# Causal attention inside a mixture-of-experts kernel: P turned by query tile, P@V in seven pieces, inverses in two groups

## The chip, the cores and the metric

The kernel runs on one core of a Trainium2 chip. The metric is the time of one execution on the device, in microseconds (us). Engines are named as the profile names them: PE (TensorE, matmuls; PEld its weight loads), DVE (VectorE), ACT (ScalarE), POOL (GpSimd), SP (SyncE, which here issues the DMAs).

## The reference

```python
# q, k, v: (2, 12, 448, 64); float32
scores = q @ k.T / 8, causal mask (-1e9 above the diagonal), minus the row's maximum
attn   = exp(scores); attn /= attn.sum(-1) + 1e-09
x      = (attn @ v) with heads side by side: (896, 768)
# soft mixture of experts, 8 experts x 4 slots
logits = x @ phi                              # (896, 32)
d      = softmax over the tokens (sum + 1e-09); slots = d.T @ x
out_e  = relu(slots_e @ w1[e]) @ w2[e]
x      = softmax over the slots (sum + 1e-09) @ out
# gated layer
out    = ((x @ w_a) * (x @ w_b)) @ w_out      # (896, 768)
```

## The kernel before

The 24 heads are worked in twelve pairs (`it` from 0 to 11). A pair's two heads lie side by side on the 128 partitions, 64 each. The 448 queries are cut into seven query tiles of 64 rows (`i` from 0 to 6); by the causal mask tile i needs 64(i+1) keys. The seven tiles are grouped into four banks, `BANKS = ((6, 0), (5, 1), (4, 2), (3,))`, and each pair is worked in four quarters (`g` from 0 to 3), one bank a quarter. The order is written out by hand: the loop over `it` and `g` at the end of the listing is the order in which each engine gets its instructions, and each engine works its own in that order.

One quarter of pair `it` does this. PE makes the scores of one bank (L266 the mask, L271 the products); DVE takes the rows' maxima (L277); ACT takes the exponentials with their sums (L292, each followed by a short read of the sum). In the first quarter PE also makes P@V of pair it-2 (`pv`, L361). In every quarter PE turns one block of four 128x128 squares of P of pair it-1 (`transp`, L321) into PSUM, from where DVE copies it to the tile pT (L328, L334). `TBLK` lists the sixteen squares (key tile kt, query tile i) in the order in which they lie in pT, and `TORD` says which block of four is turned in which quarter. A square can be turned only when its query tile has been divided by its row sums: DVE adds 1e-9 to the sums (L304) and inverts them (L305), POOL multiplies the tile by the inverses (L308). This is `norm`; it is called in the third quarter for banks 0 and 1, in the fourth for bank 2, and in the first quarter of the next pair for bank 3. In the last pair (11) it is called bank by bank.

POOL has one more task: `begin`, in the second quarter, scales the next pair's queries by 1/8 (L252), once their DMA has landed; the scores of the next pair wait for it.

Beside attention, ACT and DVE convert weights that are packed as 64-bit numbers to 32 bits, three pieces of 768 columns a pair (ACT L168 and L171, DVE L212), and SP loads the next piece into the ring as soon as one is converted. Every third pair PE also makes the logits (L385). When the first six pairs are done, `dispatch0` makes the first half of the softmax over tokens in three parts placed by `DSP`: maxima (PE L400, DVE L401, ACT L405), the turning of the exponentials (PE L411, DVE L413) and their product with x (PE L419, DVE L435). In pairs 10 and 11, and behind them, `keep` has PE multiply the identity into unused places, in counts written by hand (L340).

After attention (131 us on) come the experts, the combination and the gated layer. They load 64 pieces of w1 and w2 through the same ring, and end at 354 us.

Of the kernel before, what the change touches and what calls it, by code (L numbers as in the profile page):

```python
# [17 lines left out]
ALU = mybir.AluOpType  # L18
# [3 lines left out]
S = 448  # L22
# [3 lines left out]
BANKS = ((6, 0), (5, 1), (4, 2), (3,))  # L26
CIX = {6: 0, 0: 1, 5: 2, 1: 3, 4: 4, 2: 5, 3: 6}
POFF = []
_o = 0
for _i in range(7):  # L30
    POFF.append(_o)
    _o += 128 * ((_i + 2) // 2)
PCOLS = _o
TBLK = [(kt, i) for kt in range(4) for i in range(2 * kt, 7)]
NR = 4
NT1 = 32
WPRE = (0,5,20,25)
TORD = (1, 3, 0, 2)
KTORD = (0, 2, 3, 1)
SCQ = 1  # L40
TDVE = (0,1)
TDV2 = (2,3)
TILES = (
    (("rect", 4, 4, 0, 4), ("rect", 8, 4, 0, 8), ("rect", 12, 4, 0, 12), ("tri", 0, 4), ("sq", 0, 8)),
    (("rect", 16, 4, 0, 16), ("rect", 20, 4, 0, 13), ("tri", 4, 2)),
# [2 lines left out]
    (("sq", 8, 16),),  # L48
)
CVOFF = 6  # L50
NRAW = 2
NWARM = 32
NW2 = 4
LAG = 1
CVN = (1,1,0,1)
STAGES = (3, 5)
DSP = ((7, 3), (8, 1), (8, 2))
GROUPS = ((0, 1, 2, 3), (4, 5), (6, 7))
RPOS = (21, 31, 32, 33)
NSEL = 31  # L60
# [28 lines left out]
KEEPV = {10: 12, 11: 6}  # L89
KEEPX = 10  # L90
KEEPT = 24
KEEPE = (2, 3)
KEEPW = 5
KEEPB = (6, 20, 5, 14, 6, 8)
# [3 lines left out]
def moe_kernel(ctx: ExitStack, tc: tile.TileContext, pk, vt, phi, w1, w2, wab, wo, rsel, out):  # L98
    nc = tc.nc
# [19 lines left out]
    for h in range(2):  # L119
        blk = mask16[h * 64:(h + 1) * 64, :]  # L120
        nc.gpsimd.affine_select(
            out=blk, in_=blk, pattern=[[-1, 64]], compare_op=ALU.is_ge, fill=NEG, base=0, channel_multiplier=1,
# [107 lines left out]
    st = {}  # L230
# [54 lines left out]
    def softmax(it, g):  # L285
# [3 lines left out]
        for i, o in zip(tl, (0, 64 * (tl[0] + 1))):  # L289
# [4 lines left out]
                bias=d["nm"][:, c:c + 1], scale=d["scale"], accum_out=d["sm"][:, c:c + 1],  # L294
            )

    def norm(it, tl):
        if not tl:
            return
        d = st[it]  # L300
        lo = CIX[tl[0]]
        p, rc, sm = d["p"], d["rc"], d["sm"]
        r = rc[:, lo:lo + len(tl)]
        nc.vector.tensor_scalar(out=r, in0=sm[:, lo:lo + len(tl)], scalar1=1e-9, scalar2=None, op0=ALU.add)  # L304
        nc.vector.reciprocal(out=r, in_=r)  # L305
        for i in tl:
            n = 64 * (i + 1)
            nc.gpsimd.tensor_scalar(  # L308
                out=p[:, POFF[i]:POFF[i] + n], in0=p[:, POFF[i]:POFF[i] + n],
                scalar1=rc[:, CIX[i]:CIX[i] + 1], scalar2=1.0, op0=ALU.mult, op1=ALU.mult,  # L310
            )
# [26 lines left out]
    def keep(ps, n):  # L338
        for _ in range(n):
            nc.tensor.matmul(  # L340
                ps, lhsT=ident16[:, 0:ps.shape[0]], rhs=ident16[:, 0:ps.shape[1]], start=True, stop=True,
                skip_group_check=True,
            )

    def pv(it):
        d = st[it]
        v = d["v"]
        ps = psV.tile([128, 512], F32, tag="v", name=f"v{it}")
        keep(ps[:, S:512], KEEPV.get(it, 0))
        for kt in KTORD:  # L350
            b0 = TBLK.index((kt, 2 * kt))
            n = 7 - 2 * kt
            if (it, kt) == (10, KTORD[1]):
                keep(psX.tile([128, 128], F32, tag="x", name="idle_x"), KEEPT)
            for h in range(2):
                r = slice(64 * h, 64 * h + 64)
                if kt < 3:
                    lhsT, rhs = v[:, kt, h, :], d["pT"][:, b0:b0 + n, r]
                else:
                    lhsT, rhs = v[0:64, kt, h, :], d["pT"][0:64, b0:b0 + n, r]  # L360
                nc.tensor.matmul(  # L361
                    ps[r, 128 * kt:S], lhsT=lhsT, rhs=rhs, start=(kt == KTORD[0]), stop=(kt == KTORD[3]), skip_group_check=True
                )
        x = ap.tile([128, S], F32, tag="xT", bufs=4, name=f"xT{it}")
        nc.scalar.activation(out=x, in_=ps[:, 0:S], func=AF.Copy)
        xT[it] = x
# [154 lines left out]
    with tc.manual_schedule():  # L521
# [15 lines left out]
        for it in range(13):  # L537
            if 1 <= it < 12:
                load_v(it)
            for g in range(4):  # L540
                if it == 1:
                    warmup(NW2)
                if it < 12:
                    scores(it, g)
                if g == 0 and it >= 2:
                    pv(it - 2)
                if it >= 1:
                    transp(it - 1, TORD[g])
                if step >= CVOFF and CVN[(step + 1) % len(CVN)]:
                    conv_begin(NT1)  # L550
                if it < 12:
                    softmax(it, g)
                if g:
                    if it < 12:
                        norm(it, BANKS[g - 1] if it == 11 else ((), BANKS[0] + BANKS[1], BANKS[2])[g - 1])
                elif it:
                    norm(it - 1, BANKS[3])
                if g == SCQ and it + 1 < 12:
                    begin(it + 1)
                if g == 3 and it + 2 < 12:  # L560
                    load_qk(it + 2)
                if (it, g) in DSP:
                    dispatch0(DSP.index((it, g)))
                if it >= 2 and g == (3 if it == 8 else 1):
                    xtr(it - 2)
                if it in (4, 7, 10) and g == 2:
                    logits((it - 4) // 6, (0, 1, 2) if it != 7 else (3, 4, 5))
                step += 1
                if step > CVOFF:
                    conv_step(CVN[step % len(CVN)], LAG, NT1)  # L570
                if g in TDVE and 1 <= it < 12:
                    evict(it - 1)
# [777 lines left out]
```

## Time and profile before

| | us |
|---|---|
| median of 3 runs | 355.96 |
| lowest and highest | 354.63, 356.37 |
| the profiled execution's own time | 356.16 |
| its span in the trace | 354.1 |

The span runs from the first to the last instruction that the trace shows; what lies around it is 2.06 us. PE is busy for 330.2 us of the span, DVE 214.6, ACT 185.7, POOL 77.4. Times in the rows below are counted from the span's start.

### The profile page before, as it was taken

Reading aid. Unit: us, or ns where it says so; the run is one execution under the profiler, and the core shown is the slowest. Engines: PE = TensorE matmul, PEld = TensorE weight load, DVE = VectorE, ACT = ScalarE, POOL = GpSimd, SP = SyncE. Lnnn points to the kernel's source line nnn. Section 1 sums busy time; section 2 is a strip of 40 time slices with the busy share of each in tenths; the row PEclk is TensorE's granted clock in tenths of the full one; section 3 lists DMA queues with packets and bytes.
Section 4 is the critical chain, followed back from the end, with each engine's and each line's share of the span. In section 5 each row is a group of like instructions: output and inputs, shape, how many; then the busy total and the mean of one; then the engine's idle time right before and its main releaser. Section 6 shows DMA issues by size and latency. Waiting matters only on the chain.

```text
span 354.1 us, 6857 instructions
## 1 busy us (share of the span) xinstructions
PE 330.2 (93%) x2551; PEld 200.9 (57%) x2551; DVE 214.6 (61%) x631; ACT 185.7 (52%) x419; POOL 77.4 (22%) x128
## 2 busy tenths in 40 slices
PE   8899999999999998979987799999899999999996
PEld 5454555545555654423432346634575499989895
DVE  3589999998999842021023877607965799533221
ACT  2499989999898821013036436413644442534321
POOL 2455555554656500010000000000000000121210
PEclk9899999999999999999999989999999999999999
DMA  7759988899799797999999989787920000002122
GB/s 268 308 211 353 327 320 303 322 363 389 290 337 322 260 402 268 420 419 413 418 308 416 417 284 369 252 342 263 423 118 0 3 3 0 0 2 89 44 91 90
DMA packets 20225, 90.52 MB, mean 256 GB/s; under 512 B 2336, under 2 KB 5024, under 8 KB 20192
## 3 DMA queue, kind: packets, MB, share of 16 engines
q1 hardware_dynamic: 20192, 90.09, 67.6%
q8 instruction: 20, 0.33, 0.4%
q14 instruction: 13, 0.11, 0.1%
HBM read 87.33 MB, written 2.75 MB: 254 GB/s over the span
## 4 chain that ended last, share of the span: by engine, by line
PE 65%; DVE 15%; ACT 8%; POOL 4%; DMA 3%; issue 3%; POOLq 0%; ACTq 0%; DVEq 0%
PE M L940 11%; PE o L1240 9%; PE s L271 7%; PE h L669 5%; PE t L321 5%; PE so L710 5%; POOL p L308 4%; PE v L361 4%; DMA raw<-in_wo_dram 3%; ACT p L292 3%; PE ab L796 3%; DVE pf L879 2%; DVE pt L878 2%; PE c L1121 2%; PE hp L689 2%
## 5 line engine op out<-in xcount | busy, mean ns | idle before, releaser
L308 POOL TENSOR_SCALAR p<-p,rc 128x448 f32<-128x448 f32 (+6 forms) x84 | 58.0, 705 | 40.4 <-DVE rc L305 37.2
L271 PE MATMUL s<-qk 64*64 64x448 f32 (+6 forms) x336 | 48.3, 401 | 0.0
L292 ACT ACTIVATE p<-s,nm 128x448 f32<-128x448 f32 (+6 forms) x84 | 39.3, 476 | 13.2 <-DVE nm L282 10.1
L1130 POOL TENSOR_TENSOR cc<-gt,cc 128x512 fp32r<-128x512 f32 (+1 forms) x6 | 6.6, 1101 | 164.5 <-ACT cc L1129 164.5
L940 PE MATMUL M<-wt,P_t 128*128 128x384 f32 x168 | 35.7, 354 | 3.2 <-DVE wt L935 1.2
L321 PE MATMUL t<-ident,p 128*128 128x128 f32 x192 | 32.2, 291 | 4.8 <-POOL p L308 4.7
L277 DVE TENSOR_REDUCE nm<-s 128x1 f32<-128x448 f32 (+6 forms) x84 | 31.9, 415 | 7.4 <-PE s L271 7.1
L940 PEld LDWEIGHTS M<-wt,P_t 128*128 128x128 f32 x168 | 28.9, 191 | 12.4 <-ACT wt L934 4.8
L669 PE MATMUL h<-w,sT 128*32 128x512 f32 x192 | 29.9, 614 | 3.1 <-ACT hs L682 1.6
L321 PEld LDWEIGHTS t<-ident,p 128*128 128x128 f32 x192 | 20.5, 142 | 21.0 <-POOL p L308 10.0
L271 PEld LDWEIGHTS s<-qk 64*64 64x64 f32 x336 | 19.9, 135 | 20.9 <-issue 15.6
L935 DVE TENSOR_TENSOR wt<-wo,wt 128x384 fp32r<-128x384 f32 x48 | 23.8, 552 | 9.6 <-ACT wt L934 9.6
L934 ACT ACTIVATE wt<-wo 128x384 fp32r<-128x384 f32 x48 | 21.8, 512 | 13.5 <-PE M L940 13.1
L361 PE MATMUL v<-pT,v 128*64 128x448 f32 (+3 forms) x192 | 27.2, 398 | 0.0
L710 PE MATMUL so<-w,hpad 128*32 128x384 f32 x256 | 24.6, 493 | 0.9 <-ACT wt L934 0.4
L168 ACT ACTIVATE wab<-raw,shr 128x768 f32<-128x768 int8 x24 | 24.3, 1013 | 0.0
L212 DVE SCALAR_TENSOR_TENSOR wab<-raw,wab 128x768 uint32<-128x768 uint32 x24 | 23.7, 987 | 0.3 <-issue 0.3
L171 ACT ACTIVATE wab<-wab,shr 128x768 int32<-128x768 f32 x24 | 22.6, 941 | 0.0
L1126 DVE TENSOR_TENSOR gt<-gt,c 128x512 f32<-128x512 f32 (+2 forms) x12 | 6.5, 544 | 25.7 <-ACT gt L1125 25.7
L878 DVE TENSOR_TENSOR pt<-abt 128x192 f32<-128x192 f32 (+16 forms) x80 | 18.4, 231 | 3.3 <-ACT abt L838 2.8
L168 ACT ACTIVATE wo<-raw,shr 128x768 f32<-128x768 int8 x12 | 12.2, 1020 | 14.6 <-DMA raw<-in_wo_dram 14.6
L879 DVE TENSOR_TENSOR pf<-abt 128x12 f32<-128x12 f32 (+19 forms) x95 | 19.6, 221 | 0.0
(163 smaller groups left out, 528.7 us busy)
## 6 DMA issues: line engine op xcount, KB each, us to landing
w<-in_w_dram SPq DMA_DIRECT2D x64, 768.0 KB, 8.3
raw<-in_wab_dram SPq DMA_DIRECT2D x24, 768.0 KB, 5.8
raw<-in_wo_dram SPq DMA_DIRECT2D x12, 768.0 KB, 7.2
qk<-in_pk_dram SPq DMA_DIRECT2D x12, 448.0 KB, 5.6
v<-in_pk_dram SPq DMA_DIRECT2D x12, 192.0 KB, 5.7
out_dram<-ost SPq DMA_DIRECT2D x6, 384.0 KB, 2.3
v<-in_vt_dram SPq DMA_DIRECT2D x12, 32.0 KB, 5.5
out_dram<-ost SPq DMA_DIRECT2D x2, 192.0 KB, 1.9
```

The lines of the kernel that those rows point to most:

```text
L168: nc.scalar.activation(out=dst, in_=top, func=AF.Prelu, bias=shr[:, 0:1], scale=1.0, alpha=2.0 ** -40)
L271: nc.tensor.matmul(sb[r, o:o + n], lhsT=qT[r, 64 * i:64 * i + 64], rhs=kT[r, 0:n], start=False, stop=True, skip_group_check=True,)
L277: nc.vector.tensor_reduce(out=d["nm"][:, c:c + 1], in_=sb[:, o:o + 64 * (i + 1)], axis=AX.X, op=ALU.max, negate=True)
L292: nc.scalar.activation(out=d["p"][:, POFF[i]:POFF[i] + n], in_=sb[:, o:o + n], func=AF.Exp, bias=d["nm"][:, c:c + 1], scale=d["scale"], ac ...
L308: nc.gpsimd.tensor_scalar(out=p[:, POFF[i]:POFF[i] + n], in0=p[:, POFF[i]:POFF[i] + n], scalar1=rc[:, CIX[i]:CIX[i] + 1], scalar2=1.0, op0 ...
L321: nc.tensor.transpose(ps[:, j, :], d["p"][:, o:o + 128], ident)
L361: nc.tensor.matmul(ps[r, 128 * kt:S], lhsT=lhsT, rhs=rhs, start=(kt == KTORD[0]), stop=(kt == KTORD[3]), skip_group_check=True)
L669: nc.tensor.matmul(ps[32 * g:32 * g + 32, :], lhsT=sT[:, 0, c, :], rhs=wt[8 * e + i // 3][:, 512 * (i % 3):512 * (i % 3) + 512], start=(i ...
L710: nc.tensor.matmul(so[32 * g:32 * g + 32, 0:384], lhsT=t[:, c, :], rhs=wt[8 * e + 4 + i // 4][:, 384 * (i % 4):384 * (i % 4) + 384], start ...
L879: nc.vector.tensor_tensor(out=view(p), in0=ops[0][0], in1=ops[0][1], op=ALU.mult)
L940: nc.tensor.matmul(mps[k][h][:, 0:384], lhsT=l[:, f, :], rhs=r, start=(n == 0 and i == 0), stop=(n == 11 and i == 2))
L1240: nc.tensor.matmul(ops[t][h][:, 0:384], lhsT=hl[k // 2][:, l, k % 2, o], rhs=mhl[k][:, r, 384 * h:384 * h + 384], start=(k == 0 and i == 0 ...
```

## The change

- `TBLK` puts the sixteen squares in another order, and `TORD` turns them in the order 3, 2, 1, 0: first the four squares of query tile 6, then those of tiles 5 and 1, of 4 and 0, of 2 and 3.
- `pv` works off the list `PVL`: seven pieces for each head in place of four. A piece is one key tile with one, two or three query tiles, which lie one square or four squares apart in pT. The columns that go through are 1024 a head, before and after.
- `NORMS` has two groups: banks 0 and 1 (inverted in the third quarter, as before), and banks 2 and 3 together (in the next pair's first quarter).
- In pairs 0 to 10 the 1e-9 is added by POOL (`guard`), right behind the exponentials of the second and of the fourth quarter, and no more by DVE.
- The three parts of the first dispatch stand at (8, 0), (8, 1), (8, 3) in place of (7, 3), (8, 1), (8, 2).
- In pair 10 the 24 filling matmuls stand ahead of the sixth piece of P@V; before, ahead of the second of four.

```diff
-TBLK = [(kt, i) for kt in range(4) for i in range(2 * kt, 7)]
+TBLK = (
+    (0, 2), (0, 3), (1, 2), (1, 3), (0, 4), (1, 4), (2, 4), (0, 0), (0, 5), (1, 5), (2, 5), (0, 1), (0, 6), (1, 6),
+    (2, 6), (3, 6),
+)
+PVL = ((0, 4, 3, 4), (1, 5, 3, 4), (2, 6, 3, 4), (3, 15, 1, 1), (0, 7, 2, 4), (0, 0, 2, 1), (1, 2, 2, 1))
...
-TORD = (1, 3, 0, 2)
-KTORD = (0, 2, 3, 1)
+TORD = (3, 2, 1, 0)
...
+NORMS = ((), BANKS[0] + BANKS[1], (), BANKS[2] + BANKS[3])
...
-DSP = ((7, 3), (8, 1), (8, 2))
+DSP = ((8, 0), (8, 1), (8, 3))
...
+    def guard(it, tl):
+        if tl and EPSLO <= it < 11:
+            c = slice(CIX[tl[0]], CIX[tl[0]] + len(tl))
+            nc.gpsimd.tensor_scalar(
+                out=st[it]["rc"][:, c], in0=st[it]["sm"][:, c], scalar1=1e-9, scalar2=0.0, op0=ALU.add, op1=ALU.add
+            )
...
-        nc.vector.tensor_scalar(out=r, in0=sm[:, lo:lo + len(tl)], scalar1=1e-9, scalar2=None, op0=ALU.add)
+        if it == 11 or it < EPSLO:
+            nc.vector.tensor_scalar(out=r, in0=sm[:, lo:lo + len(tl)], scalar1=1e-9, scalar2=None, op0=ALU.add)
         nc.vector.reciprocal(out=r, in_=r)
...
-        for kt in KTORD:
-            b0 = TBLK.index((kt, 2 * kt))
-            n = 7 - 2 * kt
-            if (it, kt) == (10, KTORD[1]):
+        for kt, b0, n, by in PVL:
+            i = TBLK[b0][1]
+            if (it, b0) == (10, KEEPP):
                 keep(psX.tile([128, 128], F32, tag="x", name="idle_x"), KEEPT)
+            k = slice(0, 128 if kt < 3 else 64)
             for h in range(2):
                 r = slice(64 * h, 64 * h + 64)
...
                 nc.tensor.matmul(
-                    ps[r, 128 * kt:S], lhsT=lhsT, rhs=rhs, start=(kt == KTORD[0]), stop=(kt == KTORD[3]), skip_group_check=True
+                    ps[r, 64 * i:64 * (i + n)], lhsT=v[k, kt, h, :], rhs=d["pT"][k, b0:b0 + by * (n - 1) + 1:by, r],
+                    start=(kt == 0), stop=(b0 in (15, 7, 2)), skip_group_check=True,
                 )
...
+                if it < 12:
+                    guard(it, NORMS[g])
                 if g:
                     if it < 12:
-                        norm(it, BANKS[g - 1] if it == 11 else ((), BANKS[0] + BANKS[1], BANKS[2])[g - 1])
+                        norm(it, BANKS[g - 1] if it == 11 else NORMS[g - 1])
                 elif it:
-                    norm(it - 1, BANKS[3])
+                    norm(it - 1, BANKS[3] if it == 12 else NORMS[3])
```

What the diff does to POOL shows in the rows of one pair. These are POOL's of pair 3 before (qk_478 are the queries of pair 4, p_137 is P, rc the inverses, sm the sums; the last number is the operand's shape):

```order
L252 TENSOR_SCALAR qk_478<-qk_478 128x448
L308 TENSOR_SCALAR p_137<-p_137,rc_424 128x448
L308 TENSOR_SCALAR p_137<-p_137,rc_424 128x64
L308 TENSOR_SCALAR p_137<-p_137,rc_424 128x384
L308 TENSOR_SCALAR p_137<-p_137,rc_424 128x128
L308 TENSOR_SCALAR p_137<-p_137,rc_424 128x320
L308 TENSOR_SCALAR p_137<-p_137,rc_424 128x192
L308 TENSOR_SCALAR p_137<-p_137,rc_424 128x256
```

And the same pair after:

```order
L306 TENSOR_SCALAR rc_427<-sm_426 128x4
L258 TENSOR_SCALAR qk_477<-qk_477 128x448
L322 TENSOR_SCALAR p_137<-p_137,rc_427 128x448
L322 TENSOR_SCALAR p_137<-p_137,rc_427 128x64
L322 TENSOR_SCALAR p_137<-p_137,rc_427 128x384
L322 TENSOR_SCALAR p_137<-p_137,rc_427 128x128
L306 TENSOR_SCALAR rc_427<-sm_426 128x3
L322 TENSOR_SCALAR p_137<-p_137,rc_427 128x320
L322 TENSOR_SCALAR p_137<-p_137,rc_427 128x192
L322 TENSOR_SCALAR p_137<-p_137,rc_427 128x256
```

The first add stands ahead of the scaling of the next pair's queries, and the second between the two groups of tiles.

On PE the first quarter of pair 5 reads thus before, from the scores on (v is P@V of pair 3, t_1 the first block that is turned of pair 4; behind each row stand the engines that it waits for):

```order
L271 MATMUL s_0_721<-qk_593 64x448 [waits DMAHW2_49,Pool_49]
L271 MATMUL s_0_721<-qk_593 64x448
L271 MATMUL s_0_721<-qk_593 64x64 x2
L361 MATMUL v_729<-pT_621,v_484 64x448 [waits DMAHW6_49,DVE_49]
L361 MATMUL v_729<-pT_621,v_484 64x448
L361 MATMUL v_729<-pT_621,v_484 64x192 x2
L361 MATMUL v_729<-pT_621,v_484 64x64 [waits DMAHW7_49]
L361 MATMUL v_729<-pT_621,v_484 64x64
L361 MATMUL v_729<-pT_621,v_484 64x320 [waits DVE_49]
L361 MATMUL v_729<-pT_621,v_484 64x320
L321 MATMUL t_1_741<-ident,p_132 128x128 [waits PE_49,Pool_49]
L321 MATMUL t_1_741<-ident,p_132 128x128 x2
```

After:

```order
L277 MATMUL s_0_728<-qk_596 64x448 [waits DMAHW2_49,Pool_49]
L277 MATMUL s_0_728<-qk_596 64x448
L277 MATMUL s_0_728<-qk_596 64x64 x2
L371 MATMUL v_736<-pT_630,v_483 64x192 [waits DMAHW6_49,DVE_49]
L371 MATMUL v_736<-pT_630,v_483 64x192 x5
L371 MATMUL v_736<-pT_630,v_483 64x64 [waits DMAHW7_49]
L371 MATMUL v_736<-pT_630,v_483 64x64
L371 MATMUL v_736<-pT_630,v_483 64x128 x2
L371 MATMUL v_736<-pT_630,v_483 64x128 [waits DVE_49]
L371 MATMUL v_736<-pT_630,v_483 64x128 x3
L335 MATMUL t_3_754<-ident,p_132 128x128 [waits PE_49,Pool_49]
L335 MATMUL t_3_754<-ident,p_132 128x128 x3
```

Eight products have become fourteen, with three waits in both, and the block that is turned next is number 3 (tile 6 alone) where it was number 1 (tiles 4, 5, 6 and 2).

The first part of the dispatch has moved on PE. After the change its row stands here, in the first quarter of pair 8 (lt; before, it stood ahead of the scores of that pair, s_0):

```order
L371 MATMUL v_1099<-pT_991,v_844 64x128 x3
L335 MATMUL t_3_1117<-ident,p_137 128x128 [waits PE_49,Pool_49]
L335 MATMUL t_3_1117<-ident,p_137 128x128 x3
L411 MATMUL lt_1129<-lsb,selsum 128x448 [waits Activation_49]
L272 LDWEIGHTS ident_81
L272 MATMUL s_1_1139<-mask_83,ident_81 128x2x64
L277 MATMUL s_1_1139<-qk_957 64x384 x2
L277 MATMUL s_1_1139<-qk_957 64x128 x2
L335 MATMUL t_2_1147<-ident,p_137 128x128 [waits PE_49,Pool_49]
L335 MATMUL t_2_1147<-ident,p_137 128x128 x2
L335 MATMUL t_2_1147<-ident,p_137 128x128 [waits Pool_49]
L422 MATMUL dps_1159<-ident,lsb 112x32 [waits Activation_49]
```

Between lt and the turning of its exponentials (dps) PE now has one bank of scores and one block to turn; before, it had two banks of scores, P@V and two blocks.

## Rows read from the trace of the kernel before

**Rows 1.** Busy time by engine, granted clock and DMA, in stretches of the span.

```profile
20.72:29.54 8.82, 8.82 (x71) 4.85 (x68) 8.37 (x21) 8.66 (x22) 5.13 (x8) 1.00 0.95 349
29.54:39.05 9.51, 8.91 (x70) 4.86 (x68) 9.16 (x21) 9.12 (x24) 5.55 (x8) 1.00 0.94 341
...
49.56:58.33 8.77, 8.77 (x71) 4.87 (x68) 8.27 (x20) 7.76 (x19) 4.93 (x8) 1.00 0.88 317
...
131.00:190.00 59.00, 52.05 (x516) 23.40 (x514) 9.92 (x27) 11.51 (x18) 1.91 (x9) 1.00 0.98 378
```

**Rows 2.** What PE waited for, 5 to 131 us: total, times, longest.

```profile
PE t L321 <- POOL p L308: 4.7, 6, 1.7
```

**Rows 3.** Timeline of PE around the first quarter of pair 6.

```profile
57.25 0.65 PE L271 MATMUL s<-qk 64*64 64x256 f32 x4
...
58.48 1.08 PE L271 MATMUL s<-qk 64*64 64x448 f32 x8
59.49 2.25 PE L361 MATMUL v<-pT,v 128*64 128x448 f32 x16
62.33 0.73 PE L321 MATMUL t<-ident,p 128*128 128x128 f32 x4 [0.59 <-POOL p L308]
```

**Rows 4.** Timeline of PE at the first transposition, pair 1.

```profile
10.67 1.08 PE L271 MATMUL s<-qk 64*64 64x448 f32 x8
13.48 0.97 PE L321 MATMUL t<-ident,p 128*128 128x128 f32 x4 [1.73 <-POOL p L308]
...
14.92 1.97 PE L271 MATMUL s<-qk 64*64 64x384 f32 x8
```

**Rows 5.** Busy time as in rows 1, of the two stretches at half clock.

```profile
13.68:17.09 3.41, 3.41 (x19) 1.97 (x18) 0.84 (x2) 0.38 (x3) 1.17 (x3) 0.50 0.56 212
...
204.84:208.20 3.36, 3.36 (x11) 1.26 (x11) 3.36 (x19) 0.94 (x2) 0.00 (x0) 0.50 0.75 309
```

**Rows 6.** Timeline of DVE at the start: the first add of 1e-9.

```profile
10.51 0.17 DVE L304 TENSOR_SCALAR rc<-sm 128x4 f32<-128x4 f32 x1
```

**Rows 7.** DVE's adds by form, 5 to 131 us: total, mean ns, idle before.

```profile
L304 DVE TENSOR_SCALAR rc<-sm 128x2 f32<-128x2 f32 x14 | 4.9, 353 | 0.4 <-ACT p L292 0.3
...
L304 DVE TENSOR_SCALAR rc<-sm 128x1 f32<-128x1 f32 x12 | 1.7, 141 | 0.0
```

**Rows 8.** POOL's smallest operation, by form, 5 to 131 us.

```profile
L308 POOL TENSOR_SCALAR p<-p,rc 128x64 f32<-128x64 f32 x12 | 4.6, 383 | 0.0
```

**Rows 9.** POOL's scaling of the queries: ns shortest, median, longest.

```profile
L252 POOL TENSOR_SCALAR qk<-qk x10: 566/567/1257, 16.0 to 107.6; 128x448 f32<-128x448 f32 x10
```

**Rows 10.** Timeline of ACT, pair 5: the last sum of the second quarter.

```profile
56.90 0.21 ACT L292 ACTIVATION_READ_ACCUMULATOR p<-s,nm 128x1 f32 x1
```

**Rows 11.** Timeline of DVE, pair 5: an add, and a conversion behind it.

```profile
60.21 0.53 DVE L304 TENSOR_SCALAR rc<-sm 128x2 f32<-128x2 f32 x1
...
60.86 1.01 DVE L212 SCALAR_TENSOR_TENSOR wab<-raw,wab 128x768 uint32<-128x768 uint32 x1
```

**Rows 12.** Timeline of PE, the last pair's blocks.

```profile
122.19 1.40 PE L321 MATMUL t<-ident,p 128*128 128x128 f32 x8
...
123.86 1.17 PE L321 MATMUL t<-ident,p 128*128 128x128 f32 x8
```

**Rows 13.** Timeline of PE, DVE and ACT at the first dispatch.

```profile
78.38 0.96 PE L400 MATMUL lt<-lsb,selsum 128*128 128x448 f32 x2
...
79.93 0.60 DVE L401 TENSOR_REDUCE smalls<-lt 128x1 f32<-128x448 f32 x1
...
80.76 0.63 ACT L405 ACTIVATE lsb<-lt,smalls 128x448 f32<-128x448 f32 x1 [0.33 <-DVE smalls L428]
```

**Rows 14.** Timeline of SP's loads at the end of attention.

```profile
113.61 12.83 SPq L494 DMA_DIRECT2D w<-in_w_dram  x8
```

**Rows 15.** The chain that ended last, its longest piece.

```profile
176.78 11.54 DMA raw<-in_wo_dram
```

**Rows 16.** Timeline of POOL, pair 5's first six tiles.

```profile
58.71 3.97 POOL L308 TENSOR_SCALAR p<-p,rc 128x448 f32<-128x448 f32 x6 [2.04 <-DVE rc L305]
```

More of the change, by code (lines that the diff above doesn't have):

```diff
@@ L50 @@
 CVOFF = 6
+EPSLO = 0
 NRAW = 2
@@ L91 @@
 KEEPT = 24
+KEEPP = 0
 KEEPE = (2, 3)
@@ L349, in pv @@
         keep(ps[:, S:512], KEEPV.get(it, 0))
-        for kt in KTORD:
-            b0 = TBLK.index((kt, 2 * kt))
-            n = 7 - 2 * kt
-            if (it, kt) == (10, KTORD[1]):
+        for kt, b0, n, by in PVL:
+            i = TBLK[b0][1]
+            if (it, b0) == (10, KEEPP):
                 keep(psX.tile([128, 128], F32, tag="x", name="idle_x"), KEEPT)
+            k = slice(0, 128 if kt < 3 else 64)
             for h in range(2):
                 r = slice(64 * h, 64 * h + 64)
[L357 to L360, printed above, removed]
                 nc.tensor.matmul(
-                    ps[r, 128 * kt:S], lhsT=lhsT, rhs=rhs, start=(kt == KTORD[0]), stop=(kt == KTORD[3]), skip_group_check=True
+                    ps[r, 64 * i:64 * (i + n)], lhsT=v[k, kt, h, :], rhs=d["pT"][k, b0:b0 + by * (n - 1) + 1:by, r],
+                    start=(kt == 0), stop=(b0 in (15, 7, 2)), skip_group_check=True,
                 )
```

## The prediction

> **What bounds the kernel now.** I began with the busy time stretch by stretch, a stretch being one pair of heads. Read PE's column against the stretch's length: pair 2 takes 8.82 us with PE busy for all of it, pair 5 takes 8.77 and is full too; pair 3 does the same work and takes 9.51 with PE busy for 8.91 [rows 1]. DVE and ACT stand close behind (9.16 and 9.12 of 9.51), but where PE has no hole the pair is 0.7 us shorter, so PE's row sets the pace of attention and its holes are what can be won. Next I asked what those holes wait for. From 5 to 131 us there is one answer: the first transposition waits for POOL's division of P, six times, 4.7 us in all, the longest 1.7 [rows 2]. The timeline shows the place: scores, P@V, 0.59 us of nothing, then the turning [rows 3]. The five short holes (pairs 3, 4, 6, 7, 10) make 3.0 us together, 0.6 each; the long one is the first transposition of all [rows 4]. They arise because the block turned first holds squares of tiles 4, 5, 6 and 2, and so needs six of the seven tiles divided.
>
> The granted clock is the last view: two stretches stand at 0.50, that is 1.2 GHz in place of 2.4 [rows 5]. The first runs from 13.68 to 17.09, 0.2 us after the end of the 1.73 us in which PE stood idle [rows 4].
>
> **The change, part by part.**
>
> The first block now holds tile 6 alone, the first that POOL divides. In the quarter of rows 3 POOL begins that tile at 58.71 [rows 16]; even at 1.26 us, the longest that it takes for 448 columns [rows 9], it is done by 60.0, and PE asks for it when P@V ends, at 61.74 [rows 3]. So all five short holes close at this place: 3.0 us. The later blocks need tiles 5 and 1, then 4 and 0, then 2 and 3. The second group of inverses comes a quarter later than before, but its first square is wanted only two blocks (0.7 us each) and two banks of scores (1.08 each) after the quarter begins, 3.5 us on PE [rows 3], against a reciprocal and three POOL operations of 0.4 to 0.6 us [rows 8, 9]. I price that at nothing; a DVE that comes to the reciprocal 1.5 us late would cost what is over.
>
> At the start the hole is 1.73 us. DVE's first add began at 10.51 [rows 6]; on POOL it begins there too. The add itself is not in this trace on POOL. Bounds: not under DVE's 0.14 us [rows 7], not over POOL's smallest tile, 0.38 on average [rows 8]; I take 0.3, near the second, since it is the same engine and kind of operation with fewer columns. Then a reciprocal (as short as DVE's other small operations, 0.2), two hand-overs (0.2 to 0.3 together) and the first tile at 0.57, as the scaling of the same 448 columns [rows 9]: ready at 11.8 to 12.0. The scores end at 11.75 [rows 4]. About 0.3 us of wait stays; **1.4 us** is won.
>
> The half clock behind it: in it eight score matmuls take 1.97 us instead of 1.08 [rows 4]; the whole 3.41 us hold 1.7 us of delay [rows 5]. With no long idle ahead, the clock has no cause to fall. I take **1.6 us**, leaving 0.1 for filling matmuls that nobody waits for.
>
> The removed DVE work is three adds and one of three reciprocals a pair, about 0.8 us (0.17, 0.35 and 0.14 for the adds [rows 6, 7], 0.15 for the reciprocal by the same measure). It is off PE's path, and buys only slack on an engine that was 96% busy (9.16 of 9.51 [rows 1]). I price it at nothing; without that cover it would be worth up to 0.8 us a pair, which the full PE excludes.
>
> POOL's first add of a pair stands ahead of the scaling of the next pair's queries, and PE's next scores wait for that scaling. This is where the closed holes can partly come back. In pair 5, full as it is, ACT's last sum of the second quarter is read at 57.11 [rows 10], and the next scores that read the scaled queries start at 58.48 [rows 3]: 1.37 us. Into it go the add (0.3, bounds 0.14 and 0.38), the scaling (0.57) and hand-overs (0.1 to 0.3): 0.97 to 1.17, so it fits, with little to spare. Queued behind the add on POOL is that scaling, then the first tile; whoever waits is PE. ACT's own work is nearly a full pair long too (9.12 of 9.51), so with the holes gone it can fall somewhat further back. I charge 0.1 us for each of the five closed holes: 3.0 becomes **2.5 us**.
>
> Here a row speaks against the change: the scaling, 0.57 us as a rule, once took 1.26, and an add on DVE took 0.53 where another took 0.17, with POOL working beside it [rows 6, 9, 11]. The Trainium skill (Advanced Engine Details and Errata, VectorE Performance Modes) says why: VectorE's second port into SBUF is shared with GpSimd, so that two-port VectorE instructions and GpSimd's block each other. By that rule the adds that leave DVE stop being blocked, and the ones that come to POOL can be; the trace agrees with the blocking. I charge nothing for it in the forecast, since by the loop no conversion of DVE stands in the second quarter; it is the third rival.
>
> P@V has seven pieces a head instead of four, the columns unchanged. What a piece costs beside its columns: one piece of 256 columns takes 0.65 us, two pieces of 512 take 1.08, so 256 columns and one piece more are 0.43 [rows 3]. From this, four pieces with 1024 columns would be 1.94; P@V takes 2.25. If the 0.31 left over belongs to the four pieces, it is 0.08 a piece, three more are 0.23 a pair, 2.8 us in twelve pairs. If it belongs to the three places where PE waits for a semaphore, which are three before and after, it is nothing. Bounds 0 and 2.8; I take 0, since the waits can be read in the order of the instructions, and a price for a piece in no row by itself.
>
> The last pair's first two blocks took 1.40 us, the other two 1.17 [rows 12]; the difference is the wait for POOL that the new order drops: **0.2 us**. The filling matmuls, the loads and their counts stay.
>
> The dispatch: between the start of its first part (lt) and the turning of the exponentials PE now has 0.96 us of lt itself, scores of 1.08 and 0.7 of turning [rows 3], 2.6 us. The chain beside it is lt 0.96, DVE 0.60 and a small operation of 0.15, ACT 0.63 and a read of 0.2 [rows 7, 10, 13], 2.5 with no queue on either engine. I charge **0.2 us**; free at best, and 1 us if ACT comes a conversion late.
>
> **The sum.** 1.4 + 1.6 + 2.5 + 0.2 - 0.2 = 5.5 us. It lies wholly before 131 us and must carry to the end. From 131 to 190 us the DMAs are busy 98% [rows 1], and the longest single piece of the chain, 11.54 us, is a load [rows 15]. So the stream of weights matters there. It begins with eight loads at 113.61 [rows 14] that go out as attention's conversions free the ring: earlier attention, earlier stream. I carry all of it. The profiled execution took 356.16 us, 0.2 over the median of 355.96; taken off the median, 350.5.
>
> **Rivals.**
>
> 1. The second half-clock stretch goes as well. It is 3.36 us [rows 5], worth 1.7. For it: the three runs lie 354.63 to 356.37, 1.74 apart, as if one run had been without one such stretch. Against: the work around it is unchanged. Time 348.8.
>
> 2. The closed holes come back behind the scaling, or behind the landing of the queries' DMA; PE is then full nowhere more than before, and start, clock and tail remain: 5.5 - 2.5 = 3.0, time 353.0. For it: 0.2 us of spare. Against: a DVE with less to do reaches the maxima sooner.
>
> 3. Slower: DVE's conversions hold POOL during both add and scaling, each 0.69 us longer (1.26 less 0.57 [rows 9]). The 1.0 to 1.2 us become 2.4 to 2.6 against 1.37: 1.1 us on each of ten pairs, 11 us, against the 3.0 that closed holes give and 3.0 from start, clock and tail: 361. It decides against the kernel from 0.6 us a pair. Against: DVE's conversions come in the other three quarters, so only a DVE that has drifted would do it.
>
> 4. P@V pays for its pieces, 2.8 us: 353.3.
>
> 5. The stream of weights, not attention, sets the rest: no change, 356. For it: the 98%. Against: in attention the DMAs move 317 to 349 GB/s, and 378 behind it [rows 1], so they wait there for the ring.
>
> **How the numbers follow.** A measurement of this kernel tells about 0.5% (1.8 us) from no change. Forecast 0.50, rival 1 0.15, rival 2 0.13, rival 4 0.08, rival 5 0.07, slower 0.07. Forecast and rivals 1, 2, 4 are faster by over 1.8 us, save the edges of 2 and 4: 0.84. Same 0.09, slower 0.07. The range leaves out rivals 3 and 5 and a little of each edge: 348.2 to 353.7. The likeliest case alone spans 349.5 to 351.8, from the bounds of the start, the scaling and the dispatch.
>
> **What would show it.** PE's waits for POOL at the transposition gone, or 0.3 us at the first; the stretch from 13 to 17 us at full clock; pairs without logits at 8.8 to 8.9 us all along; P@V still about 2.25 us; lt and its turning without a hole between them over 0.3 us; the experts beginning some 5.5 us sooner and the 11.5 us load no longer. It is wrong if PE shows new waits ahead of a pair's first scores, if P@V grows, or if the experts start early and end no earlier.

## The result, and the profile after

The changed kernel took 350.78 us (median of 4 runs, 349.99 to 351.46) against 355.38 (354.63 to 356.37) beside it: a ratio of 0.9868, interval 0.9831 to 0.9906. Measured twice more in the sets below, the same kernel gave 0.9892 (0.9855 to 0.9928) and 0.9882 (0.9843 to 0.9921), so the change is worth 1.1 to 1.3%, 3.8 to 4.7 us. Executions that lie over 1.5% above the fastest of their kernel are left out of ratios and medians: one of the kernel before (359.11) and one of the changed kernel (354.49), both in the sets below. The profiled execution took 351.46 with a span of 349.4; before it was 356.16 and 354.1.

First PE's waits from 5 to 131 us (total, times, longest), against [rows 2]. In the changed kernel L335 is the turning of P, L277 the scores, L258 POOL's scaling of the queries, L411 and L422 lt and the turning in the dispatch:

```profile
PE s L277 <- POOL qk L258: 1.1, 1, 1.1
PE dps L422 <- ACT es L416: 0.9, 1, 0.9
PE s L277 <- DMA qk<-in_pk_dram: 0.4, 1, 0.4
PE lt L411 <- ACT lsb L401: 0.2, 1, 0.2
```

The turning waits for POOL nowhere. New are a wait of 1.1 us ahead of a pair's scores and one of 0.4 for pair 1's queries. (The 0.9 stands behind the last pair, and was there before.) The stretches of pairs 2 to 5 and of the experts, to be read as [rows 1]:

```profile
17.73:26.52 8.79, 8.79 (x83) 5.60 (x81) 8.10 (x18) 8.79 (x22) 5.77 (x11) 1.00 0.97 350
26.52:36.47 9.95, 8.86 (x83) 5.59 (x81) 9.40 (x20) 9.67 (x25) 6.73 (x11) 1.00 0.94 342
36.47:46.24 9.77, 9.77 (x86) 5.77 (x87) 8.50 (x17) 9.25 (x22) 6.77 (x11) 1.00 0.97 352
46.24:55.03 8.79, 8.79 (x82) 5.60 (x81) 7.73 (x17) 7.91 (x20) 5.27 (x11) 1.00 0.92 340
131.00:190.00 59.00, 52.89 (x497) 22.38 (x500) 10.23 (x24) 14.75 (x23) 1.91 (x9) 0.97 1.00 388
...
13.68:17.09 3.41, 3.41 (x35) 2.18 (x31) 2.95 (x9) 2.36 (x10) 1.89 (x5) 1.00 0.55 205
177.03:180.44 3.41, 3.07 (x20) 0.99 (x24) 1.86 (x3) 2.18 (x3) 0.00 (x0) 0.50 1.00 290
200.92:204.33 3.41, 3.41 (x11) 1.75 (x12) 3.06 (x14) 0.94 (x2) 0.00 (x0) 0.50 0.73 221
```

These stretches, from a pair's first scores to the next pair's, begin at the product; those of [rows 1] begin 0.15 us earlier, at the mask. The first and the fourth are full at 8.79 us; 9.77, in the third, is a pair with logits, and full too; the second has the new hole. The lower three rows answer to [rows 5]: the stretch that stood at half clock now has the full 1.00, and behind 131 us there are two stretches at half clock where there was one.

PE's timeline: the first transposition, against [rows 4]; pair 6's first quarter, against [rows 3]; the last pair, against [rows 12]; the first matmul of the experts (L682):

```profile
10.90 1.08 PE L277 MATMUL s<-qk 64*64 64x448 f32 x8 [0.41 <-DMA qk<-in_pk_dram]
11.91 0.66 PE L335 MATMUL t<-ident,p 128*128 128x128 f32 x4
...
12.78 1.08 PE L277 MATMUL s<-qk 64*64 64x384 f32 x8
...
55.03 1.08 PE L277 MATMUL s<-qk 64*64 64x448 f32 x8
56.04 2.26 PE L371 MATMUL v<-pT,v 128*64 128x192 f32 x28
58.24 0.66 PE L335 MATMUL t<-ident,p 128*128 128x128 f32 x4
...
116.88 1.09 PE L335 MATMUL t<-ident,p 128*128 128x128 f32 x8
...
118.31 1.16 PE L335 MATMUL t<-ident,p 128*128 128x128 f32 x8
...
132.59 2.78 PE L682 MATMUL h<-w,sT 128*32 128x512 f32 x24
```

The transposition follows the scores without a hole, 1.57 us sooner than at 13.48 and at full clock. P@V takes 2.26 us for 28 matmuls where 16 took 2.25. The experts begin at 132.59; before, the same matmul began at 138.13. That is 5.54 us sooner, where the sum said 5.5.

The chain that ended last (start, length, what) shows where the new hole comes from, and what became of the gain behind 131 us:

```profile
27.65 7.66 DMA qk<-in_pk_dram
...
35.46 0.96 POOL qk L258
36.42 0.04 issue
36.47 1.08 PE s L277 x8
...
171.23 12.36 DMA raw<-in_wo_dram
```

Pair 4's queries land 7.66 us after their issue; only then can POOL scale them, and the scores wait for that. The load that was the chain's longest piece, 11.54 us [rows 15], is issued 5.55 us sooner and takes 12.36, so it lands 4.73 us sooner. 4.7 is also what the span has lost: 0.8 of the 5.5 us is given back here. The row from 131 to 190 doesn't say why, since before, its first 7.1 us lie ahead of the experts. Counted from the first expert matmul, in the form of [rows 1], first before and then after, up to the load's issue and while it is under way:

```profile
138.13:176.78 38.65, 35.56 (x332) 15.39 (x333) 4.00 (x13) 5.85 (x10) 1.91 (x9) 1.00 1.01 415
176.78:188.32 11.54, 10.20 (x112) 4.09 (x113) 2.85 (x4) 3.13 (x3) 0.00 (x0) 1.00 1.02 333
...
132.59:171.23 38.64, 35.55 (x332) 15.39 (x333) 4.00 (x13) 5.85 (x10) 1.91 (x9) 1.00 1.01 415
171.23:183.59 12.36, 10.62 (x101) 4.02 (x102) 2.83 (x4) 3.21 (x3) 0.00 (x0) 0.86 1.02 332
```

The DMAs are as busy and move data at the same rate in both, so fuller DMAs are not what makes the load longer. What differs in these rows is the granted clock, 0.86 in place of 1.00: the new stretch at half clock, from 177.03, lies within the load.

### The profile page after: what moved, and what is told of

Same layout as the page of the kernel before. It is cut to its first block, busy times and chain, and to the rows that moved or that the text cites. A ratio compares the mean times of both kernels' runs of the same rounds, so it can differ in the third digit from the quotient of the medians.

```text
span 349.4 us, 7132 instructions
## 1 busy us (share of the span) xinstructions
PE 329.3 (94%) x2695; PEld 209.2 (60%) x2695; DVE 207.8 (59%) x587; ACT 184.7 (53%) x419; POOL 83.7 (24%) x150
## 4 chain that ended last, share of the span: by engine, by line
PE 72%; DVE 12%; DMA 8%; ACT 4%; issue 1%; POOL 1%; SPq 1%; ACTq 0%; DVEq 0%; POOLq 0%
PE M L953 12%; PE s L277 10%; PE o L1253 9%; PE v L371 7%; PE t L335 6%; PE h L682 5%; PE so L723 5%; DMA qk<-in_pk_dram 4%; DMA raw<-in_wo_dram 4%; PE ab L809 3%; DVE pf L892 2%; DVE pt L891 2%; PE c L1134 2%; PE hp L702 2%; DVE pf L903 2%; PE xt L384 1%
## 5 line engine op out<-in xcount | busy, mean ns | idle before, releaser
L322 POOL TENSOR_SCALAR p<-p,rc 128x448 f32<-128x448 f32 (+6 forms) x84 | 59.0, 718 | 10.9 <-DVE rc L319 10.2
L277 PE MATMUL s<-qk 64*64 64x448 f32 (+6 forms) x336 | 47.2, 394 | 1.6 <-POOL qk L258 1.1
L277 PEld LDWEIGHTS s<-qk 64*64 64x64 f32 x336 | 19.6, 133 | 22.0 <-issue 15.0
L682 PE MATMUL h<-w,sT 128*32 128x512 f32 x192 | 29.9, 613 | 2.1 <-ACT hs L695 1.6
L335 PE MATMUL t<-ident,p 128*128 128x128 f32 x192 | 31.1, 286 | 0.0
L371 PE MATMUL v<-pT,v 128*64 128x192 f32 (+2 forms) x336 | 27.4, 299 | 0.0
L335 PEld LDWEIGHTS t<-ident,p 128*128 128x128 f32 x192 | 20.1, 141 | 11.4 <-issue 7.1
L371 PEld LDWEIGHTS v<-pT,v 128*64 128x64 f32 (+1 forms) x336 | 19.2, 135 | 6.0 <-issue 2.8
L809 PE MATMUL ab<-wab,sT 128*32 128x384 f32 x192 | 20.0, 523 | 0.5 <-DVE sT L647 0.5
```

The source lines that it names most:

```text
L277: nc.tensor.matmul(sb[r, o:o + n], lhsT=qT[r, 64 * i:64 * i + 64], rhs=kT[r, 0:n], start=False, stop=True, skip_group_check=True,)
L322: nc.gpsimd.tensor_scalar(out=p[:, POFF[i]:POFF[i] + n], in0=p[:, POFF[i]:POFF[i] + n], scalar1=rc[:, CIX[i]:CIX[i] + 1], scalar2=1.0, op0 ...
L335: nc.tensor.transpose(ps[:, j, :], d["p"][:, o:o + 128], ident)
L371: nc.tensor.matmul(ps[r, 64 * i:64 * (i + n)], lhsT=v[k, kt, h, :], rhs=d["pT"][k, b0:b0 + by * (n - 1) + 1:by, r], start=(kt == 0), stop= ...
L682: nc.tensor.matmul(ps[32 * g:32 * g + 32, :], lhsT=sT[:, 0, c, :], rhs=wt[8 * e + i // 3][:, 512 * (i % 3):512 * (i % 3) + 512], start=(i ...
L809: nc.tensor.matmul(abps[q][32 * g:32 * g + 32, 0:384], lhsT=sT[:, 1, c, :], rhs=w[:, c % 2, 384 * g:384 * g + 384], start=(c == 0), stop=( ...
```

## The experiments

No kernel here leaves out any of the work. Ratios are to the kernel before, beside them on the same chip: the first four are one set (before 354.49), the next three another (354.24), the last four a third (356.06).

**The order of the squares alone** (`TBLK`, `TORD`, `PVL` as changed; the rest as before):

```diff
-EPSLO = 0
+EPSLO = 11
-NORMS = ((), BANKS[0] + BANKS[1], (), BANKS[2] + BANKS[3])
+NORMS = ((), BANKS[0] + BANKS[1], BANKS[2], BANKS[3])
-DSP = ((8, 0), (8, 1), (8, 3))
+DSP = ((7, 3), (8, 1), (8, 2))
```

Expected: 

> The new order of turning and the seven pieces alone: 1e-9 added by DVE, inverses in three groups and the dispatch as before. Theory (PE sets the pace, and its holes came from the block that was turned first): PE waits for POOL at the transposition no more than 0.3 us in all, the stretch behind 13 us at full clock, the experts' first matmul at 132.5 to 133.3 us (138.1 before, 132.6 after the whole change), time 350.3 to 351.6 us. Rival (DVE, 96% busy, has to be relieved of its adds for the holes to close): holes of 0.3 us or more in most pairs, the experts begin at 135 us or later, time 353 us or more.

Measured: 351.2 us, ratio 0.987 (0.9822 to 0.9917), and no wait of the turning for POOL (`EPSLO = 11` leaves the adds on DVE). The experts begin at 133.46, a little later than expected; PE waits twice for the scaling of the queries, 1.3 us in all. That is the whole gain. The adds, the two groups and the place of the dispatch add nothing that can be told.

**Everything but the order** (old `TBLK`, `TORD`, four pieces; adds on POOL, new dispatch). The old first block needs tile 2 of bank 2, which two groups would divide too late; so this kernel keeps three groups, and POOL makes three adds a pair:

```diff
-TORD = (3, 2, 1, 0)
+TORD = (1, 3, 0, 2)
-NORMS = ((), BANKS[0] + BANKS[1], (), BANKS[2] + BANKS[3])
+NORMS = ((), BANKS[0] + BANKS[1], BANKS[2], BANKS[3])
```

Expected: 

> The whole change but for the order of turning, which with its four pieces is as before; inverses in three groups, since the old order needs tiles 4 and 2 a quarter earlier; 1e-9 by POOL, dispatch at the new quarters. Theory: the holes at the first transposition are back, six or more, 4.5 to 6 us in all, with half clock after the first; experts begin at 137.5 to 138.7 us, time 354.5 to 356.5 us, though DVE has less to do. Rival (relief of DVE): holes under 0.3 us each, experts begin at 133 to 135.5 us, time 351 to 353 us.

Measured: 375.62 us, ratio 1.0543 (1.0476 to 1.0611). I had not foreseen 20 us of loss. PE's waits, in the view of the first fence (L332 is here the turning, L319 POOL's scaling of P):

```profile
PE t L332 <- POOL p L319: 16.5, 9, 2.7
```

Before, it was 4.7 in six [rows 2]. POOL's timeline in pair 3 (L303 is the add of 1e-9, L255 the queries):

```profile
32.84 0.56 POOL L255 TENSOR_SCALAR qk<-qk 128x448 f32<-128x448 f32 x1
34.66 0.42 POOL L303 TENSOR_SCALAR rc<-sm 128x2 f32<-128x2 f32 x1 [1.26 <-ACT p L295]
35.17 2.67 POOL L319 TENSOR_SCALAR p<-p,rc 128x448 f32<-128x448 f32 x4
37.92 0.23 POOL L303 TENSOR_SCALAR rc<-sm 128x1 f32<-128x1 f32 x1
38.25 2.16 POOL L319 TENSOR_SCALAR p<-p,rc 128x320 f32<-128x320 f32 x3
```

POOL stands idle for 1.26 us until ACT has the sums of bank 2, with the four tiles of banks 0 and 1 queued behind the add; DVE had made their inverses by 34.1, so they lose the last 0.5 us of it and the add's own time. Then the add of bank 3 (37.92) stands ahead of the two tiles of bank 2, which the turning is waiting for. The turning starts at 39.60 after 2.05 us of nothing. There is more half clock too: the granted clock is 0.50 from 14.42 for 6.83 us, and from 51.97, 86.10 and 120.24 for 3.41 each; before there was one such stretch ahead of 131 us. 11.8 us more of waits, and half of 13.7 us more at half clock, make 18.6; the experts begin 20.0 us later than before (158.17).

**The same with the adds behind the scaling** in POOL's queue, to test that reading:

```diff
-                if it < 12:
-                    guard(it, NORMS[g])
                 if g:
...
                     norm(it - 1, BANKS[3] if it == 12 else NORMS[3])
+                if it < 12:
+                    guard(it, NORMS[g])
```

Expected: 

> The old order of turning with three groups and the adds on POOL (375.6 us), with one thing changed: each add stands in POOL's queue behind the scaling of the bank before it, not ahead of it. The same instructions, in another order on one engine. Theory: of the 20 us most come from the queue: the add of bank 3 waits for ACT's sums (1.26 us idle at 34.66) with four ready tiles behind it, and the next add stands ahead of the two tiles that the transposition wants. With the adds behind, the hole falls from 2.05 us to between 0.6 (as with the adds on DVE) and 1.3, the clock stays full in attention, and the time is 355 to 364. Rival: the way from POOL over DVE's reciprocal and back to POOL costs the time, wherever the add stands: then the hole stays near 2 us and the time above 370.

Measured: 357.66 us, ratio 1.0112 (1.0035 to 1.0189), the hole 1.03 us, and the clock full from 4.85 to 161.87. The turning still waits 7.5 us in eight waits. (The add that waits for ACT's sums at 34.66 is that of bank 2.) The same instructions in another order on one engine are worth some 18 of the 20 us, what half clock costs among them: the theory holds. The hole keeps 0.4 us over before's 0.59 [rows 3]; the way from POOL over DVE's reciprocal and back has a price too.

**The new order with three groups on POOL**, the fourth corner:

```diff
-NORMS = ((), BANKS[0] + BANKS[1], (), BANKS[2] + BANKS[3])
+NORMS = ((), BANKS[0] + BANKS[1], BANKS[2], BANKS[3])
```

Expected: 

> The changed kernel, but with the inverses in three groups (the third bank, tiles 4 and 2, apart from the fourth, tile 3), so that POOL has three adds a pair, and the add of the fourth bank stands in POOL's queue ahead of the scaling of tiles 4 and 2. With the old order of turning the same groups and adds gave 375.6 us and nine waits of the transposition for POOL. Theory: those waits came because the block turned first needed tiles 4 and 2; in the new order they are wanted only by the third and fourth block, two quarters later, so no transposition waits and the time is that of the changed kernel, 350 to 353. Rival: three adds on POOL are slow by themselves, because its queue waits for ACT's sums three times a pair and the scaling of the queries is behind it: then the next scores wait, a pair takes 10 us or more, and the time is above 358.

Measured: 350.22 us, ratio 0.9867 (0.9819 to 0.9915), no wait of the turning. (Pair 1's scores wait 1.58 us for their queries and a stretch at half clock follows, from 11.72; the experts begin at 133.70.) What costs 20 us under the old order costs nothing under the new one, since the late tiles are wanted two quarters later.

**The adds back on DVE** (`EPSLO = 11`, the rest as changed):

```diff
-EPSLO = 0
+EPSLO = 11
```

Expected: 

> The whole change, but 1e-9 is added by DVE in all pairs, in two groups. Theory: DVE is off PE's path, so nothing changes by more than 0.4 us: experts begin at 132.3 to 133.0 us, time within 0.7 us of the whole change run beside it. Rival (DVE's adds blocked by POOL reach PE, 0.4 to 0.8 us a pair in eleven pairs): experts begin 2 us or more later, time 353 us or more.

Measured: 349.99 us, ratio 0.9852 (0.9806 to 0.9899), against 0.9892 (0.9855 to 0.9928) for the changed kernel beside it: the intervals overlap. The median is 1.6 us lower and the experts begin at 131.69, sooner than I expected (0.7 us and 132.3): in this profile the hole at pair 4 is 0.3 us. That the adds on POOL cost something is not shown, nor excluded.

**The changed kernel again**, in that set:

Expected: 

> The whole change once more, unaltered, to see what repeats. The experts should begin at 132.4 to 132.8 us again; the time should lie at 350 to 351.5 us. If the spread behind 131 us goes with stretches at half clock, the runs with the lower mean clock are the longer ones, 1.7 us for each 3.4 us stretch; if they are off the path, the clock says nothing of the time.

Measured: 351.55 us (348.74 to 353.7, 9 runs). The executions with the lower mean clock are the longer ones: 348.81 us at 1.0, 348.74 to 350.53 at 0.995, 351.55 to 352.13 at 0.990, 352.41 and 353.7 at 0.985. (The ten others of this kernel, those of the result and of its third run, are less well ordered: 349.99 to 351.35 at 0.988, 354.21 at 0.990.) The profiled execution was the longest, 353.7, and shows one way in which executions differ: PE's timeline at the start,

```profile
9.71 0.22 PE L272 MATMUL s<-mask,ident 128*128 128x128 bf16 x1
11.49 1.37 PE L277 MATMUL s<-qk 64*64 64x448 f32 x4 [1.56 <-DMA qk<-in_pk_dram]
```

and the stretch behind it, as in [rows 5]:

```profile
11.93:15.34 3.41, 3.41 (x21) 2.12 (x19) 1.69 (x5) 1.02 (x4) 1.56 (x5) 0.50 0.96 369
```

Pair 1's queries came 1.56 us late and the clock fell; the experts begin at 134.76, 2.17 us later than in the first profile. So the half clock at the start can still come, by another wait; it did so in two more profiles, of the kernels with three groups and with the load moved.

**The first hole filled** in the kernel before:

```diff
                 if it == 1:
                     warmup(NW2)
...
+                if (it, g) == (1, 0):
+                    warmup(28)
                 if it >= 1:
                     transp(it - 1, TORD[g])
```

Expected: 

> The kernel before, with nothing changed but 28 filling matmuls on PE ahead of the first transposition, where PE stood idle for 1.73 us (11.75 to 13.48); four such matmuls take 0.22 us at full clock, so they take about 1.55 us and fit. They move no work. The term of the sum for the clock says that the stretch at half clock from 13.68 to 17.09 comes from that idle time and costs 1.6 us: then the stretch goes, the first transposition still starts near 13.5, and the first expert matmul starts 1.4 to 1.7 us sooner than before's 138.13, near 136.6. Rival: the stretch has another cause, or its delay is made up for by the holes behind it: then the half clock stays, or it goes and the first expert matmul starts within 0.5 us of 138.1. Total: 353.5 to 355 against 354.5 to 355.5, too near to tell by the median alone; the trace decides.

Measured: ratio 0.9986 (0.9957 to 1.0014). PE's timeline (L527 the filling, L321 the turning, L669's matmul of the experts now L671):

```profile
11.89 1.74 PE L527 MATMUL warm<-ident 128*128 128x128 bf16 x28
13.47 0.61 PE L321 MATMUL t<-ident,p 128*128 128x128 f32 x4
...
136.16 2.35 PE L671 MATMUL h<-w,sT 128*32 128x512 f32 x20
```

The turning starts where it did, the clock is full from 4.99 to 202.96; pair 2's first quarter begins at 19.08 in place of 20.72, 1.64 us sooner, and the experts 1.97 us sooner, a little more than expected. The price of the stretch, 1.6, was right; that the median does not show it fits a stretch that only some executions of the kernel before have. Of its 36 executions in the three sets, 20 have a mean clock of 0.995 or 1.0 and a median of 354.27; 12 have 0.990 and a median of 356.77; the other four lie from 354.07 to 356.41. The profiled one of [rows 5], two stretches at half clock, is of the second kind (0.990, 356.16). Of the ten with the hole filled, nine have 0.995 or 1.0. Only the mean clock is known of executions without a profile, not where a stretch stood.

**A load of weights three loads later**, for the new hole:

```diff
-WPRE = (0,5,20,25)
+WPRE = (0,8,20,25)
```

Expected: 

> The changed kernel with one early load of expert weights put three loads later in SP's queue. In the profile of the changed kernel pair 4's scores wait 1.16 us, because the load of its queries is issued at 27.65 behind that load of weights (22.73) and a load for the conversions, and lands only at 35.31, 7.66 us later. Theory: with 768 KB less ahead of them the queries land about 2 us sooner, the hole at pair 4 falls from 1.16 us to under 0.3, and the first expert matmul starts up to 1 us sooner for it; the time falls by 0 to 1.2 us against the changed kernel beside it. Rival: the load moved stands in another load's way (the queries of pair 5) and the hole moves there: PE's waits for POOL's scaling stay at 1 us or more, and the time is the same.

Measured: 351.06 us against 351.19 for the changed kernel beside it. The hole at pair 4 is gone and a hole of 1.09 us stands at pair 7, whose queries land 7.61 us after their issue. The time is the same, as the rival has it. That the move brought the hole to pair 7 is not shown: the next kernel has it there without the move, and the last profile of the changed kernel has none. Here pair 1's scores also wait, 1.81 us, with half clock from 12.18, and the experts begin at 135.13.

**The dispatch back at its old quarters**:

```diff
-DSP = ((8, 0), (8, 1), (8, 3))
+DSP = ((7, 3), (8, 1), (8, 2))
```

Expected: 

> The changed kernel with the three parts of the first dispatch at the quarters where they stood before (last of pair 7, second and third of pair 8). The sum charged 0.2 us for their move; the profile after shows a hole of 0.23 us there. By the sum the hole goes and the time falls by 0.2, which is within what can be told: 0.3 us either way against the changed kernel beside it. Rival: in the old place, at full PE, lt and the reading of its maximum stand in the way of a pair's first maxima on DVE and PE waits there: slower by 0.5 us or more.

Measured: 350.15 us, ratio 0.9847 (0.9815 to 0.9879), against 0.9882 (0.9843 to 0.9921) beside it. The median is 1.04 us lower, where I expected 0.3 either way, but the intervals overlap: not to be told apart. Pairs 7 and 8 take 21.54 us together, less the hole of 1.09 that this profile has there, against 21.64 in the run below; the move costs 0.1 us of PE. In the same pair the late queries show what happens next on POOL and DVE:

```profile
62.38 1.28 POOL L258 TENSOR_SCALAR qk<-qk 128x448 f32<-128x448 f32 x1 [0.81 <-DMA qk<-in_pk_dram]
```

```profile
62.30 0.93 DVE L218 SCALAR_TENSOR_TENSOR wab<-raw,wab 128x768 uint32<-128x768 uint32 x1
```

The scaling, 0.57 us as a rule, takes 1.28 when it starts beside a conversion. The Trainium skill (Advanced Engine Details and Errata, VectorE Performance Modes) says that GpSimd and two-port VectorE instructions block each other at the shared port. These rows show POOL held up beside a DVE instruction; that this one is of the two-port kind, no run here shows.

**Queries of pair 1 first, the load later, adds on DVE**:

```diff
-        load_v(0)
-        pump(2)
         load_qk(1)
-        pump(2)
+        load_v(0)
+        pump(4)
...
-WPRE = (0,5,20,25)
+WPRE = (0,8,20,25)
-EPSLO = 0
+EPSLO = 11
```

Expected: 

> An attempt at a faster version: the changed kernel with the load of weights put later as in the run beside it, the load of pair 1's queries ahead of pair 0's V and of the first two loads for the conversions, and the adds of 1e-9 on DVE as before the change. In the profiles of the changed kernel pair 1's scores wait for those queries, 0.4 us in one and 1.6 in the other, and the longer wait was followed by a stretch at half clock from 11.93. Theory: both waits go, no execution has half clock before 131 us, and the median is 1 to 2.5 us under that of the changed kernel beside it, 348.5 to 350. Rival: the waits of the start are paid back when the conversions begin, which now get their data later: same time as the changed kernel.

Measured: 349.84 us (348.81 to 350.62), ratio 0.9835 (0.9805 to 0.9866). The wait for pair 1's queries is gone, the clock is full from 6.03 to 152.80, one wait for the scaling of 0.4 us is left, and the experts begin at 131.14. It is the lowest median of that set, but the interval overlaps with the changed kernel's: 1.35 us better by the medians, not shown to be faster.

**The changed kernel, third time**:

Expected: 

> The changed kernel once more, beside the other three on the same chip: 350 to 352, the measure for them. Its profile tells again which waits repeat: pair 4's scores for the late queries (1.1 us in two profiles), pair 1's for theirs (0.4 and 1.6), and the stretches at half clock near 177 and 201 (in two profiles).

Measured: 351.19 us (349.95 to 354.21). Here pair 1's scores wait 0.97 us without a fall of the clock, and no pair waits for late queries: five pairs without logits take 8.78 to 8.86 us, and the nine pairs from 2 to 10 take 85.2 where the kernel before took 88.5. The stretches near 177 and 201 are there again.

## Why the prediction was right, point by point

**The closed holes, 2.5 us.** Right in cause: the order of the squares alone gives the whole gain, and with no late queries (the third profile) the nine pairs win 3.3 us. In the first profile they win 2.2, from 88.47 us (20.87 to 109.34) to 86.27 (17.73 to 104.00). What comes back was of the wrong form: I charged 0.1 us in each of five pairs for the add and the scaling. There are no such delays. There is one hole of 1.1 us in one pair, when its queries land late, rival 2's second cause; it shows in four profiles of the changed kernel and its near kin (pair 4 twice, pair 7 twice), and in shorter form in others. The changed kernel itself had it at pair 4 in two profiles and nowhere in the third.

**The first hole, 1.4.** Measured 1.57: the whole 1.73 us of waiting went, with none of the 0.3 that I had left, and the scores ahead end 0.16 later. Nothing hangs on the engine of the add: with it on DVE the first transposition starts at 12.04 (order alone) or 11.91 (adds back), and with it on POOL at 11.91. The add took 0.24 us on POOL (estimate 0.3).

**The clock, 1.6.** Right for the profiled execution: from the first transposition to pair 2's scores the work took 5.82 us against 7.39, 1.57 less, and the filled hole alone gave 1.64 by the same point. As a term of a median it was too large, since the stretch comes in a part of the executions only. The median that I took it from, of three runs, had two that lay above 355.9; by the 36 executions it is 354.57, and the 5.5 us of the profile are 3.8 to 4.7 between medians. That the forecast of 350.5 lies so near the 350.78 is partly luck: it started 1.4 us too high and took off 0.8 to 1.7 too much. The reason that I gave, no long idle ahead, covers this one hole only; pair 1's queries can make another.

**Rival 1** said that the stretch behind 200 us would go; it stayed. What it is worth, 1.7 by that rival, stays open. With the hole filled, five executions at 0.995 have a median of 354.52 and four at 1.0 one of 354.53, as if it were nothing; but the nine executions of the changed kernel, run again, get longer as the mean clock falls, and the figures of the last section put it between 1.1 and 2.0.

**Nothing for the pieces, the second group and DVE's relief.** 2.26 us for 28 matmuls; no difference that can be told between two and three groups under the new order, nor between the adds on either engine. The forecast of nothing fits all three. Rival 3, conversions that hold POOL, is seen only when the queries are late, and in one pair, not in ten.

**The last pair 0.2, the dispatch 0.2.** The first two blocks took 1.09 us after 1.40 [rows 12], 0.3 won; the move of the dispatch costs 0.1 to 0.2.

**All of it carried to the end.** Up to 131 us the sum was met, 5.54 for 5.5. Of it 4.7 arrived: the load of w_out, which was to be no longer, takes 0.82 us more. By the rows above, the rate is no reason, 333 and 332 GB/s, so this is no point for rival 5. Of the profiles whose chain holds this load, six with a stretch at half clock inside it took 11.86 to 12.76 us, five without 10.54 to 11.92. But the clock cannot be all of it: at 174.50, ahead of the stretch, PE already waits 0.61 us for weights, where before it waited 0.21 at the same place (179.65). Why the loads land later stays open.

## What to carry to other kernels

Before work is made faster, ask which of its results is wanted first: the order in which squares were turned was worth all of the gain, and moving or removing the operations ahead of them nothing that could be told. An instruction that waits holds all that is ready behind it on its engine: the same adds cost nothing or 18 us by where they stood in POOL's queue and how soon the tiles behind them were wanted. A term that is read from one profile belongs to that execution; look at the mean clock of the other runs before it goes into a median.

## What was not expected of the hardware

Half clock follows a hole in some places and not in others, though the holes are alike. At the start, holes of 1.73 us (before), 1.56 (changed, second profile), 1.58 (three groups) and 1.81 (load moved) were followed by 3.41 us at half clock; 1.59 us in the run with the adds behind, and 0.97 in the third profile, were not. It is so within one execution too: with everything but the order, waits of 2.04 to 2.05 us that end at 50.58, 84.88 and 120.22 were followed by half clock from 51.97, 86.10 and 120.24, and those as long that end at 39.60 and 73.91 were not. Stretches at half clock in the experts do not all cost the same: from the first expert matmul to the start of the last matmul of the output the profiles took 211.4 to 211.8 us where one stretch stood between 152 and 183, though it was 6.8 us long in two of them, 212.1 to 212.5 with one behind 200, and 212.9 to 213.4 with both. So a stretch behind 200 us, beside an earlier one, went with 1.1 to 2.0 us more, about what half clock for its length would cost; an earlier one of double length cost no more than a single one. That DMA, not the clock, sets the earlier part is an argument from these rows; no run tested it.
